# Four leading attention units recast in two 64-token halves, in a planned kernel of linear attention and two MoE layers

## The chip, the cores and the metric

The kernel runs on one core of a Trainium2 chip. The metric is the device time of one execution in microseconds (us), the median of several runs. A profile of one further execution is read beside it; its times count from the start of the profiled span.

## What is computed

```python
def _attn_ref(q, k, v):                      # q, k, v: (2, 8, 768, 64), float32
    ...
    for t in range(S):
        state = gamma[None, :, None, None] * state + np.einsum('bhd,bhe->bhde', k[:, :, t], v[:, :, t])
        y[:, :, t] = scale * np.einsum('bhd,bhde->bhe', q[:, :, t], state)
...
def _moe_ref(x, w_in, w_out):                # x: (1536, 512), w_in: (512, 2048), w_out: (2048, 512)
    h = x @ w_in
    g = np.maximum(h, 0.0) + np.log1p(np.exp(-np.abs(h)))
    return (g @ w_out).astype(np.float32)
...
def _moe2_ref(x, w_in, w_out):
    h = x @ w_in
    relu6 = np.clip(h + 3.0, 0.0, 6.0)
    return ((h * relu6 / 6.0) @ w_out).astype(np.float32)
```

The attention output, turned to (1536, 512), is x of the first layer, whose output is x of the second. The weights come as float64; the kernel turns their 64-bit words into float32 itself.

## The kernel before

**Units.** Attention is cut into 12 units of 128 tokens (all 8 heads), six per batch. Units 0 to 3 (`START`, line 158) give the first 512 tokens, which is the first chunk of x; they stand at the head of the program, and no GEMM can begin before all four are done. Units 4 to 11 run later, two at a time, between GEMMs. A unit's steps on TensorE are named in the planner's table (line 280): Tk and Tq transpose k and q with the identity; S makes the scores, D the product of k and v that feeds the running state, I the part of the output inside the unit, C the part that the carried state adds. In units 0 to 3, S is 8 matmuls of 64 x 128 x 128 (one per head), and I and D 8 each; unit 0 has no C (`attend`, lines 677 to 741). The later units, in pairs, halve their 128 tokens and use 64 x 64 x 64 matmuls, one on each quadrant of the array: `pair`, lines 743 to 829. There the state is added up twice per unit, to a middle state and an end state, and C multiplies both.

Between TensorE's steps, ScalarE (ACT) copies kT out of PSUM and rounds x to `x_hi` (line 738); VectorE (DVE) scales q and v (`qT`, `vs`), masks the scores (`pw`), adds up the state (`st`), reads two columns between two accumulations (`seen`), and makes the low part `x_lo` (line 739).

**Weights.** A block of weights takes one load of raw words (512 KB, tile `raw`) and a row of steps (`Words.made`, line 392): ACT `bits` (`cv<-raw,half`), `sign` (`cv<-raw`) and `scale` (`raw<-raw`), DVE clamp (`raw<-raw`, one or two instructions) and merge (`cv<-raw,cv`), ACT rounding to the high part (`w<-cv`) and DVE the low part (`w<-cv,w`). This text calls the blocks raw_0, raw_1, ... in the order of their loads; the first four go to the weight tiles w_77, w_78, w_79, w_80, and raw_4 to w_81. The buffers number the other way: `raw_0_68` holds raw_0 and later a sixth block, raw_5, and so on.

**GEMMs.** A G1 is twelve 128 x 128 x 512 matmuls of three products (high times high, high times low, low times high), a G2 the same with the second weights. Behind a G1, ACT copies `g` out of PSUM and the softplus follows on DVE and ACT, up to `hi` and `lo`, which the G2 of that block reads.

**Order.** A planner (`Plan.run`, line 75) writes the whole program down in order: each step has a cost, a due time, what it must follow and the buffers it takes, and it picks the next step per engine by earliest start and due time. Due times come from the list of TensorE steps and their costs (lines 284 to 327). A load may carry `hold`, a planned time before which it isn't placed; `HOLD` (line 171) is added to it for the later units (line 627). The chip knows neither: each engine runs its instructions in the written order and waits on semaphores. All loads of the head and the ramp go through SP's queue.

```python
 284      pe = [("Tk", 0), ("Tq", 0)]
 285      for u in range(START):
 286          pe += [("S", u)] + [("C", u)] * (u % (S // P) > 0) + [("D", u)] + ([("Tk", u + 1), ("Tq", u + 1)] if u + 1 < START else []) + [("I", u)]
```

Of the kernel before, what the change touches and what calls it, by code (L numbers as in the profile page):

```python
# [10 lines left out]
F32 = mybir.dt.float32  # L11
# [7 lines left out]
P = 128  # L19
# [126 lines left out]
def kernel(ctx, tc, q, k, v, w1_in, w1_out, w2_in, w2_out, table, out):  # L146
# [7 lines left out]
    C = P  # L154
# [16 lines left out]
    HOLD = 7.0  # L171
# [108 lines left out]
    cost = {"Tk": 0.46, "Tq": 0.46, "S": 0.60, "D": 0.60, "C": 0.98, "I": 0.60, "S0": 0.97, "D0": 0.57, "I0": 0.97, "C0": 0.97, "SS": 1.3, "DD": 1.25, "II": 1.3, "CC": 2.0, "G1": GEMM, "G2": GEMM, "unit": UNIT}  # L280
# [4 lines left out]
    for u in range(START):  # L285
        pe += [("S", u)] + [("C", u)] * (u % (S // P) > 0) + [("D", u)] + ([("Tk", u + 1), ("Tq", u + 1)] if u + 1 < START else []) + [("I", u)]
# [118 lines left out]
    def weight(o, f, number):  # L405
# [19 lines left out]
        t5 = x.made(use - tail, begin + 15 if number < 1 else use - tail - 8.0, 1.45 if o else 1.5 if number < EARLY else 1.75, [x.raw_k], BY_ACT(number))  # L425
# [176 lines left out]
    def attend(u):  # L602
# [71 lines left out]
        o = [("o", u)]  # L674
        dk = ("ds", u)

        def scores(g):
            for p in range(NP):
                nc.tensor.matmul(bank(sc[g])[:, p, :], tile_of("kT")[part[g], p, :], tile_of("qT")[part[g], p, :])

        def all_scores(x):
            for p in range(NP)[ps(x)]:
                for g in range(2):
                    nc.tensor.matmul(bank(sc[g])[:, p, :], tile_of("kT")[part[g], p, :], tile_of("qT")[part[g], p, :])

        def masked(g):
            return lambda: nc.vector.tensor_tensor(tile_of("pw")[:, g], bank(sc[g]),
                                                   full.rearrange("p (n t) -> p n t", n=1).to_broadcast([P, NP, C]), ALU.mult)

        def product():  # L690
            for p in range(NP):
                for g in range(2):
                    nc.tensor.matmul(banks[part[g], nc.slot[dk][1], p * D:(p + 1) * D], tile_of("k")[:, 2 * p + g, :], tile_of("vs")[:, 2 * p + g, :])
# [516 lines left out]
```

## Time and profile before

| what | value |
|---|---|
| time, median of 3 runs | 565.89 us (565.6 to 568.1) |
| the profiled execution's own time | 566.38 us |
| its span, first to last instruction | 564.6 us |
| TensorE (PE) busy | 555.7 us, 98% of the span |
| VectorE (DVE) busy | 438.8 us, 78% |
| ScalarE (ACT) busy | 367.2 us, 65% |
| DMA moved | 100.51 MB, mean 178 GB/s |
| granted TensorE clock | full in all 40 slices |

PE busy counts pipelined matmuls whose ends are modelled, so it tells where PE had work, not how well it was used. The shares are means over very different stages: the head (about 26 us), the ramp in which the first weight blocks are made, and the long middle. Where an edit touches the head alone, the rows of the head and of the ramp behind it are the ones to read.

### The profile page before, as it was taken

To read this page: it belongs to the slowest core of one execution; us is meant where nothing else is said; L and a number is where in the kernel's file an instruction comes from. 1 tells how busy PE (TensorE), PEld (TensorE's weight loads), DVE (VectorE), ACT (ScalarE), POOL (GpSimd) and SP (SyncE) were. 2 spreads that over 40 slices of the span, in tenths; PEclk is the share of its full clock that TensorE was granted. 3 is DMA by queue.
4 is the path that set the end of the run, shared out by engine and by line. 5 is a ranking of instruction groups with operands and counts; after the bars stand their busy time and mean duration, and the time that the engine had idled before them with its cause. 6 is when DMAs were issued, how large, how long until landed. Compare 5 with 4: busy or idle time off the path is not lost.

```text
span 564.6 us, 9538 instructions
## 1 busy us (share of the span) xinstructions
PE 555.7 (98%) x3685; PEld 477.1 (84%) x3685; DVE 438.8 (78%) x778; ACT 367.2 (65%) x600; POOL 6.0 (1%) x13
## 2 busy tenths in 40 slices
PE   7999999999999999999999999999999999999997
PEld 6787888888888888888888899889998899988895
DVE  5999988889699778989998875846888887854343
ACT  4698999998574545576977943548688865432220
POOL 0000000000000000000000000000000000000000
PEclk9999999999999999999999999999999999999999
DMA  9997999996211226796936622151757652226003
GB/s 202 283 268 257 271 280 284 323 253 212 80 56 61 71 93 206 227 320 239 326 157 231 238 90 75 57 205 37 253 195 240 245 186 76 74 89 247 1 0 113
DMA packets 80477, 100.51 MB, mean 178 GB/s; under 512 B 41008, under 2 KB 57648, under 8 KB 80432
## 3 DMA queue, kind: packets, MB, share of 16 engines
q1 hardware_dynamic: 79424, 98.45, 54.1%
q0 software_dynamic: 720, 1.31, 1.4%
q8 instruction: 29, 0.48, 0.3%
q10 hardware_dynamic: 288, 0.14, 0.1%
q14 instruction: 16, 0.13, 0.1%
HBM read 74.98 MB, written 23.59 MB: 175 GB/s over the span
## 4 chain that ended last, share of the span: by engine, by line
PE 82%; DVE 8%; DMA 5%; ACT 3%; issue 1%; SPq 0%; DVEq 0%; ACTq 0%
PE banks L45 82%; DMA raw<-in_moe_w_in_dram 2%; DVE lo L45 2%; DVE g L45 1%; ACT cv L45 1%; DMA g<-stash_h 1%; DMA raw<-in_moe_w_out_dram 1%; DVE raw L45 1%; DVE xf L45 1%; DMA v<-in_v_dram 1%; ACT raw L45 1%; DVE cv L45 1%; DVE e L45 1%; ACT hi L45 1%; DVE w L45 0%
## 5 line engine op out<-in xcount | busy, mean ns | idle before, releaser
L45 PE MATMUL banks<-w,parts 128*128 128x512 f32 x579 | 136.7, 390 | 0.0
L45 PEld LDWEIGHTS banks<-w,parts 128*128 128x128 f32 x579 | 108.0, 188 | 21.3
L45 PE MATMUL banks<-hi,w 128*128 128x512 f32 x384 | 124.9, 393 | 0.0
L45 PE MATMUL banks<-xf,w 128*128 128x384 f32 x672 | 123.3, 337 | 0.4 <-DVE c L45 0.4
L45 PEld LDWEIGHTS banks<-xf,w 128*128 128x128 f32 x672 | 118.2, 188 | 3.6 <-DVE c L45 0.7
L45 PEld LDWEIGHTS banks<-hi,w 128*128 128x128 f32 x384 | 72.1, 188 | 15.2
L45 PE MATMUL banks<-xl,w 128*128 128x512 f32 x342 | 80.8, 391 | 0.0
L45 PEld LDWEIGHTS banks<-xl,w 128*128 128x128 f32 x342 | 63.8, 188 | 13.4
L45 PE MATMUL banks<-lo,w 128*128 128x512 f32 x192 | 74.8, 390 | 0.0
L45 ACT ACTIVATE e<-c,three 128x384 f32<-128x384 f32 (+1 forms) x32 | 24.6, 770 | 47.1 <-DVE c L45 46.8
L45 ACT ACTIVATE cv<-raw,half 128x512 uint32<-128x512 uint32 x64 | 48.4, 760 | 7.5 <-DMA raw<-in_moe_w_in_dram 5.0
L45 ACT ACTIVATE cv<-raw 128x512 f16<-128x512 int32 x64 | 50.2, 791 | 1.3
L45 ACT ACTIVATE e<-e 128x512 f32<-128x512 f32 x48 | 30.1, 628 | 22.9 <-DVE e L45 22.7
L45 DVE SCALAR_TENSOR_TENSOR cv<-raw,cv 128x512 uint32<-128x512 uint32 x64 | 43.8, 688 | 1.1
L45 PE MATMUL banks<-x_hi,w 128*128 128x512 f32 x128 | 42.5, 399 | 1.3 <-ACT x_hi L45 1.3
L45 PEld LDWEIGHTS banks<-lo,w 128*128 128x128 f32 x192 | 36.1, 188 | 7.0
L45 DVE TENSOR_SCALAR raw<-raw 128x512 f32<-128x512 f32 x76 | 32.0, 424 | 11.3 <-ACT raw L45 10.4
L45 ACT ACTIVATE parts<-c 128x768 fp32r<-128x768 f32 x32 | 27.0, 844 | 18.8 <-DVE c L45 18.8
L45 DVE TENSOR_TENSOR c<-total,banks 128x384 f32<-128x384 f32 x16 | 8.9, 554 | 35.1 <-PE banks L45 34.9
L45 DVE TENSOR_TENSOR parts<-c,parts 128x768 fp32r<-128x768 f32 x32 | 30.6, 957 | 7.0 <-ACT parts L45 6.5
L45 DVE SCALAR_TENSOR_TENSOR g<-g,e 128x512 f32<-128x512 f32 x48 | 32.8, 686 | 4.0 <-ACT e L45 3.8
L45 DVE TENSOR_TENSOR lo<-g,hi 128x512 fp32r<-128x512 f32 x48 | 32.8, 685 | 3.7 <-ACT hi L45 3.4
(95 smaller groups left out, 683.5 us busy)
## 6 DMA issues: line engine op xcount, KB each, us to landing
raw<-in_moe_w_in_dram SPq DMA_DIRECT2D x32, 512.0 KB, 5.7
raw<-in_moe_w_out_dram SPq DMA_DIRECT2D x32, 512.0 KB, 5.7
w<-stash_out SPq DMA_DIRECT2D x32, 512.0 KB, 5.3
stash_out<-raw SPq DMA_DIRECT2D x16, 512.0 KB, 3.4
w<-parts_out SPq DMA_DIRECT2D x14, 512.0 KB, 5.8
parts_out<-w SPq DMA_DIRECT2D x8, 512.0 KB, 5.2
stash_h<-hs SPq DMA_DIRECT2D x16, 256.0 KB, 2.0
g<-stash_h SPq DMA_DIRECT2D x16, 256.0 KB, 4.8
```

The source lines that it names most:

```text
L45: return self.plan.tc.keep_in_program_order(getattr(self.engine, op)(*args, **kwargs))
```

## The change

It makes six edits. (1) Units 0 to 3 go through the code of the pairs (now `group`), one unit at a time: halves of 64 tokens, quadrant matmuls, one mask instruction of 512 columns per unit instead of two, a middle state and one more state addition per unit; I comes first and C accumulates onto it, in unit 0 too (for its second half). (2) The planner's costs and TensorE list follow. (3) The low part of x is written over the two-bank form right behind the rounding. (4) `HOLD` falls from 7 to 4. (5) The load of raw_0 gets a due time 10 us later among the loads of the head. (6) Unit 3's last state scaling is due 15 us later, and its qT is preferred.

```diff
-    HOLD = 7.0
+    HOLD = 4.0
...
-    cost = {... "S": 0.60, "D": 0.60, "C": 0.98, "I": 0.60, "S0": 0.97, "D0": 0.57, "I0": 0.97, "C0": 0.97, ...}
+    cost = {... "S": 0.62, "D": 0.62, "C": 1.02, "I": 0.62, ...}
...
-        pe += [("S", u)] + [("C", u)] * (u % (S // P) > 0) + [("D", u)] + ([("Tk", u + 1), ("Tq", u + 1)] if u + 1 < START else []) + [("I", u)]
+        pe += [("S", u), ("D", u)] + ([("Tk", u + 1), ("Tq", u + 1)] if u + 1 < START else []) + [("I", u), ("C", u)]
...
-        t += cost.get(key[0] + "0" if key[0] in "SDIC" and key[-1] < START else "", cost[key[0]])
+        t += cost[key[0]] / (1 + (key == ("C", 0)))
...
-        t5 = x.made(use - tail, begin + 15 if number < 1 else use - tail - 8.0, ...)
+        t5 = x.made(use - tail, begin + 25 if number < 1 else use - tail - 8.0, ...)
...
-        if u >= START:
-            ready["in", u] = kt[0], qt[0], vs, ik[0]
-            if u % 2:
-                pair(u - 1, task)
-            return
...
+        ready["in", u] = kt, qt, vs, ik
+        if u in [START - 1]:
+            for t in qt:
+                t.ahead = 0.6
+        if u < START:
+            group([u], task)
+        elif u % 2:
+            group([u - 1, u], task)
...
-        def all_scores(x):
-            for p in range(NP)[ps(x)]:
-                for g in range(2):
-                    nc.tensor.matmul(bank(sc[g])[:, p, :], tile_of("kT")[part[g], p, :], tile_of("qT")[part[g], p, :])
...
+        def scores(ps):
             for x, w in enumerate(us):
+                for p in ps:
                     for j in range(2):
                         for g in range(2):
                             nc.tensor.matmul(sub(sc, g, x)[part[j], p, :], at_slot(("kT", w))[part[g], p, part[j]], at_slot(("qT", w))[part[g], p, part[j]])
...
-                then = ready["end", w] = task("DVE", 0.42, faded, [then, ready["t"]], d["DD"] + 2.2 + 1.2 * x, give=[("end", w)])
+                then = ready["end", w] = task("DVE", 0.42, faded, [then, ready["t"]], d[E] + 2.2 + 1.2 * x + 15 * (w == START - 1), give=[("end", w)])
...
+        if head:
+            def x_at(part):
+                return split(x_of(part, 0)[:, :, u * C:(u + 1) * C])
+
+            need = min(due["G1", 0], d[I] + 12.0)
+            o2 = task("ACT", PSX, lambda: nc.scalar.activation(x_at("hi"), both(o, 0), AF.Copy), [c], need - 1.5, give=o)
+            o3 = task("DVE", PSX, lambda: nc.vector.tensor_tensor(x_at("lo"), both(o, 0), x_at("hi").bitcast(F32), ALU.subtract), [o2], need - 0.8, give=o)
+            ready["x", u] = [o2, o3]
+            return
```

**ACT ahead of the first GEMM.** These are the rows up to the rounding of unit 3's x, and of the first two weight blocks. Before, from the rounding of unit 2's x on:

```order
L45 ACTIVATE x_hi_291<-banks 128x4x128
L45 ACTIVATE cv_1_74<-raw_1_69,half 128x512
L45 ACTIVATE cv_1_74<-raw_1_69 128x512
L45 ACTIVATE raw_1_69<-raw_1_69 128x512
L45 ACTIVATE cv_2_75<-raw_2_70,half 128x512
L45 ACTIVATE cv_2_75<-raw_2_70 128x512
L45 ACTIVATE x_hi_291<-banks 128x4x128
L45 ACTIVATE w_78<-cv_1_74 128x512
```

and now:

```order
L45 ACTIVATE x_hi_343<-banks 128x2x4x64
L45 ACTIVATE cv_1_74<-raw_1_69,half 128x512
L45 ACTIVATE cv_1_74<-raw_1_69 128x512
L45 ACTIVATE raw_1_69<-raw_1_69 128x512
L45 ACTIVATE cv_2_75<-raw_2_70,half 128x512
L45 ACTIVATE w_77<-cv_0_73 128x512
L45 ACTIVATE x_hi_343<-banks 128x2x4x64
L45 ACTIVATE w_78<-cv_1_74 128x512
```

The three steps of raw_1 and the first of raw_2 stay ahead of unit 3's rounding; the second of raw_2 has moved behind it, and the rounding of w_77, which stood ahead of unit 2's, is in its place.

**SP's loads.** From unit 1's v to the sixth weight block, before:

```order
L45 DMA v_1_141<-in_v_dram 128x8x64
L45 DMA raw_0_68<-in_moe_w_in_dram 128x4x256
...
L45 DMA v_3_152<-in_v_dram 128x8x64
L45 DMA raw_1_69<-in_moe_w_in_dram 128x4x256
L45 DMA raw_2_70<-in_moe_w_in_dram 128x4x256
L45 DMA words_in_112<-cv_0_73 128x512
L45 DMA raw_3_71<-in_moe_w_out_dram 128x1024
L45 DMA raw_4_72<-in_moe_w_in_dram 128x4x256
L45 DMA raw_0_68<-in_moe_w_out_dram 128x1024
L45 DMA k_0_137<-in_k_dram 128x8x64
L45 DMA q_0_134<-in_q_dram 128x8x64
```

and now, from unit 2's v:

```order
L45 DMA v_2_142<-in_v_dram 128x8x64
L45 DMA raw_0_68<-in_moe_w_in_dram 128x4x256
...
L45 DMA raw_1_69<-in_moe_w_in_dram 128x4x256
L45 DMA raw_2_70<-in_moe_w_in_dram 128x4x256
L45 DMA k_0_137<-in_k_dram 128x8x64
L45 DMA q_0_134<-in_q_dram 128x8x64
L45 DMA raw_3_71<-in_moe_w_out_dram 128x1024
L45 DMA raw_4_72<-in_moe_w_in_dram 128x4x256
L45 DMA v_0_140<-in_v_dram 128x8x64
L45 DMA k_1_138<-in_k_dram 128x8x64
L45 DMA q_1_135<-in_q_dram 128x8x64
L45 DMA raw_0_68<-in_moe_w_out_dram 128x1024
```

raw_0 has moved behind unit 2's three loads, with unit 3's three still behind it. raw_1 and raw_2 keep their place. k and q of unit 4 (in the buffers `k_0`, `q_0`) now stand ahead of raw_3, and v of unit 4 with k and q of unit 5 ahead of raw_5; the store `words_in_112` has gone behind them.

**The first G2, on PE and DVE.** PE from the end of unit 3 into the ramp, in pieces of the difference (k_0 is unit 4's k, k_1 and q_1 are unit 5's):

```order
+L45 MATMUL banks<-qT_1_146,st_167 64x64 x8
 L45 MATMUL banks<-ident,k_0_137 128x128 x4
+L45 MATMUL banks<-x_hi_343,w_77 128x512 x8
...
-L45 MATMUL banks<-x_hi_291,w_81 128x512
...
+L45 MATMUL banks<-x_hi_343,w_79 128x512
 L45 MATMUL banks<-ident,k_1_138 128x128 x4
+L45 MATMUL banks<-ident,q_1_135 128x128 x4
 L45 MATMUL banks<-hi_94,w_80 128x512
 L45 MATMUL banks<-lo_96,w_80 128x512
...
+L45 MATMUL banks<-x_hi_343,w_81 128x512
```

DVE up to the low part that this G2 reads, before:

```order
L45 TENSOR_SCALAR e_90<-g_91 128x512
L45 TENSOR_SCALAR raw_4_72<-raw_4_72 128x512 x2
L45 TENSOR_TENSOR w_80<-cv_3_76,w_80 128x512
L45 SCALAR_TENSOR_TENSOR cv_0_73<-raw_4_72,cv_0_73 128x512
L45 SCALAR_TENSOR_TENSOR g_91<-g_91,e_90 128x512
L45 TENSOR_SCALAR e_89<-g_92 128x512
L45 TENSOR_TENSOR w_81<-cv_0_73,w_81 128x512
L45 TENSOR_TENSOR lo_96<-g_91,hi_94 128x512
```

and now:

```order
L45 TENSOR_SCALAR e_90<-g_91 128x512
L45 TENSOR_TENSOR vs_0_147<-v_0_140,small 128x512
L45 TENSOR_TENSOR w_80<-cv_3_76,w_80 128x512
L45 TENSOR_SCALAR e_89<-g_92 128x512
L45 SCALAR_TENSOR_TENSOR g_91<-g_91,e_90 128x512
L45 TENSOR_TENSOR qT_0_145<-banks,tq_sb 128x512
L45 TENSOR_SCALAR raw_4_72<-raw_4_72 128x512 x2
L45 SCALAR_TENSOR_TENSOR cv_3_76<-raw_4_72,cv_3_76 128x512
L45 TENSOR_TENSOR lo_96<-g_91,hi_94 128x512
```

On PE, Tk of unit 4 has moved from behind two GEMMs to ahead of the first, and the G2 of w_80 (behind Tk and Tq of unit 5) to ahead of the G1 of w_81. On DVE its low part `lo_96` still stands last, behind raw_4's clamps and merge, and behind `vs` and `qT` of unit 4, which came later before.

## Rows read from the trace of the kernel before

**Rows 1.** Stages: us, then busy us per engine; last PEclk, DMA share, GB/s
```profile
12.00:26.00 14.00, 13.03 (x208) 11.09 (x206) 13.15 (x28) 9.02 (x14) 0.00 (x0) 1.00 1.06 265
...
26.00:60.00 34.00, 33.70 (x369) 27.38 (x370) 32.28 (x65) 31.66 (x54) 0.39 (x1) 1.00 0.90 262
60.00:200.00 140.00, 140.00 (x1299) 114.91 (x1298) 117.69 (x209) 110.68 (x186) 4.48 (x5) 1.00 0.63 189
```

**Rows 2.** Timeline of PE, unit 3 and the first GEMM (start, us, ...)
```profile
21.33 1.16 PE L45 MATMUL banks<-qT,kT 64*128 64x128 f32 x16
22.42 1.09 PE L45 MATMUL banks<-qT,st 64*64 64x128 f32 x16
23.44 0.69 PE L45 MATMUL banks<-vs,k 128*64 128x64 f32 x16
23.96 1.07 PE L45 MATMUL banks<-pw,vs 128*64 128x128 f32 x16
26.30 2.11 PE L45 MATMUL banks<-x_hi,w 128*128 128x512 f32 x8 [1.27 <-ACT x_hi L45]
```

**Rows 3.** Timeline of PE, S and C of the pair of units 4 and 5
```profile
44.82 1.16 PE L45 MATMUL banks<-qT,kT 64*64 64x64 f32 x64
...
56.94 2.08 PE L45 MATMUL banks<-qT,st 64*64 64x64 f32 x64
```

**Rows 4.** Timeline of ACT, ahead of the first GEMM and at the first softplus
```profile
22.02 0.77 ACT L45 ACTIVATE cv<-raw,half 128x512 uint32<-128x512 uint32 x1
...
25.03 0.79 ACT L45 ACTIVATE cv<-raw 128x512 f16<-128x512 int32 x1
25.68 0.57 ACT L45 ACTIVATE x_hi<-banks 128x512 fp32r<-128x512 f32 x1
26.14 0.62 ACT L45 ACTIVATE w<-cv 128x512 fp32r<-128x512 f32 x1
26.66 0.67 ACT L45 ACTIVATE raw<-raw 128x512 f32<-128x512 f32 x1
...
34.60 0.63 ACT L45 ACTIVATE hi<-g 128x512 fp32r<-128x512 f32 x1
```

**Rows 5.** Timeline of SP: issues of raw_1 with raw_2, and of raw_3
```profile
16.05 1.79 SPq L45 DMA_DIRECT2D raw<-in_moe_w_in_dram  x2
...
18.45 0.43 SPq L45 DMA_DIRECT2D raw<-in_moe_w_out_dram  x1
```

**Rows 6.** DMA issues at 16.0 and at 18.4 us: KB, us to landing
```profile
raw<-in_moe_w_in_dram SPq DMA_DIRECT2D x1, 512.0 KB, 5.9
...
raw<-in_moe_w_out_dram SPq DMA_DIRECT2D x1, 512.0 KB, 7.0
```

**Rows 7.** Timeline of PE in the ramp: Tk of unit 5, first G2, third G2
```profile
38.28 0.66 PE L45 MATMUL banks<-ident,k 128*128 128x128 f32 x4
38.70 0.48 PE L45 MATMUL banks<-hi,w 128*128 128x512 f32 x1
...
50.28 0.39 PE L45 MATMUL banks<-lo,w 128*128 128x512 f32 x1
```

**Rows 8.** Timeline of DVE in the ramp: first and third low part, mask, states
```profile
35.42 0.68 DVE L45 TENSOR_TENSOR lo<-g,hi 128x512 fp32r<-128x512 f32 x1
36.02 0.42 DVE L45 TENSOR_SCALAR raw<-raw 128x512 f32<-128x512 f32 x1
...
46.18 1.22 DVE L45 TENSOR_TENSOR pw<-banks,small 128x1024 f32<-128x1024 f32 x1
...
49.19 0.68 DVE L45 TENSOR_TENSOR lo<-g,hi 128x512 fp32r<-128x512 f32 x1
...
50.13 0.86 DVE L45 TENSOR_TENSOR st<-st,banks 128x256 f32<-128x256 f32 x2
```

**Rows 9.** Two stretches: around the first GEMM, and in the ramp
```profile
24.00:28.00 4.00, 2.73 (x29) 2.21 (x24) 3.85 (x9) 3.97 (x7) 0.00 (x0) 1.00 1.08 368
...
40.00:50.00 10.00, 10.00 (x149) 7.97 (x147) 10.00 (x20) 9.62 (x17) 0.00 (x0) 1.00 0.86 304
```

More of the change, by code (lines that the diff above doesn't have):

```diff
@@ L686, in masked @@
[L686 to L693, printed above, removed]
-        def inner():
-            for p in range(NP):
-                for g in range(2):
-                    nc.tensor.matmul(bank(o[0])[part[g], p, :], tile_of("vs")[:, 2 * p + g, :], tile_of("pw")[:, g, p, :],
-                                     **(dict(start=(p == 0), stop=(p == NP - 1)) if first else dict(start=False, stop=True, skip_group_check=True)))
@@ L701, in between @@
-        def between():
-            nc.vector.tensor_copy(seen, bank(o[0])[:, 0, :2])
-        def carry():
-            for p in range(NP):
-                for g in range(2):
-                    nc.tensor.matmul(bank(o[0])[part[g], p, :], at_slot(("end", u - 1))[part[g], p, :], tile_of("qT")[part[g], p, :],
-                                     start=(p == 0), stop=(p == NP - 1))
-        def added():
-            return banks[:, nc.slot[dk][1], :NP * D].rearrange("p (n t) -> p n t", n=NP)
-        def total():
-            nc.vector.tensor_tensor(at_slot(("end", u)), at_slot(("end", u - 1)), added(), ALU.add)
@@ L716, in faded @@
-        def faded():
-            nc.vector.tensor_tensor(at_slot(("end", u)), added() if first else at_slot(("end", u)),
-                                    tc_sb.rearrange("p (n o) -> p n o", o=1).to_broadcast([P, NP, D]), ALU.mult)
-        s = [task("PE", cost["S0"] / parts, lambda x=x: all_scores(x), [kt[x], qt[x]], d["S"] + x / 10, take=[] if x else [("bank", x) for x in sc], give=[("kT", u)] + [("qT", u)] * first) for x in range(parts)]
-        pt = [task("DVE", PSX, masked(g), s, d["I"] - 1.8 + g * 0.6, take=[] if g else own("pw"), give=[sc[g]]) for g in range(2)]
@@ L732, in attend @@
-        c = task("PE", cost["I0"], inner, pt + [vs, n], d["I"], take=[("bank", o[0])] if first else [],
-                 give=[("pw", u), ("vs", u)])
-        def x_at(part):
-            return x_of(part, 0)[:, :, u * C:(u + 1) * C]
-        need = min(due["G1", 0], d["I"] + 12.0)
-        o2 = task("ACT", PSX, lambda: nc.scalar.activation(x_at("hi"), bank(o[0]), AF.Copy), [c], need - 1.5, give=o)
-        o3 = task("DVE", PSX, lambda: nc.vector.tensor_tensor(x_at("lo"), bank(o[0]), x_at("hi").bitcast(F32), ALU.subtract), [o2],
-                  need - 0.8, give=o)
@@ L741, in attend, with group @@
-        ready["x", u] = [o2, o3]
-    def pair(u, task):
+        ready["in", u] = kt, qt, vs, ik
[6 more added lines that the diff above has]
+            group([u - 1, u], task)
+    def group(us, task):
+        u, head = us[0], us[0] < START
         ph = int(u >= FIRST)
-        us = u, u + 1
-        d = {n: due[n, u] for n in ("SS", "DD", "II", "CC")}
+        S, E, I, R = "SDIC" if head else ("SS", "DD", "II", "CC")
+        d = {n: due[n, u] for n in (S, E, I, R)}
```

53 lines of the change are left out of this document (20 added, 33 removed).

## The prediction

> **What bounds the kernel now.** I read the busy time by stage first [rows 1]: from 60 us to 200 us TensorE has work for 140.00 of 140.00 us, from 26 to 60 us for 33.70 of 34.00. Once the first GEMM has begun, PE never stands still for long, and the end comes one PE program after that start. So the change can move the end in two ways: by when the first GEMM begins, and by PE stalls that it takes away or makes behind it. Second, the timeline of PE in the head [rows 2]: the first GEMM begins at 26.30, after 1.27 us without work, and what it waited for was ACT's rounding of unit 3's x, not PE. Third, ACT [rows 4]: that rounding ran at 25.68, behind a row of weight steps that began at 22.02. Fourth, why not sooner: the load of raw_1, the first of those steps' input, was issued at 16.05 [rows 5] and took 5.9 us [rows 6], so it landed at 21.95. The head therefore ends on this chain: landing of raw_1, ACT's queue, x_hi, first GEMM. PE's own head work was nearly as long (busy 13.03 of 14 us [rows 1]), but was not the last to arrive. Fifth, the ramp: from 40 to 50 us DVE was busy for 10.00 of 10.00 us and ACT for 9.62 [rows 9]; behind the start stands a second limit, close below PE.
>
> **PE's work in the head.** From start to start a unit took S 1.09, C 1.02, D 0.52, and I 1.07 by its duration [rows 2], together 3.70. In the pair's form S of two units lasts 1.16 and C 2.08 [rows 3]; one unit is half: S 0.58, C 1.04, and I and D at 0.58, since they have as many quadrant matmuls as S. That is 2.78, a saving of 0.92 for each of units 1 to 3, 2.8 in all. Unit 0 loses 2.68 (S, D, I) and gets 1.74 plus half a C (0.52): 0.4 less. PE's head shrinks by 3.2 us. What covers it: nothing on PE; the time turns into waiting, since the chain above does not run through it. DVE's head work changes little: one mask of 512 columns less per unit, one state addition more.
>
> **The start of the first GEMM.** raw_1 keeps its place in SP's order, behind the loads of all four units and raw_0. I leave its landing at 21.95. ACT's queue then holds the same four weight steps, and in place of raw_2's sign step (25.03 to 25.68, 0.65) the rounding of w_77, which took 0.52 of the queue in w_78's case (26.14 to 26.66) [rows 4]. x_hi comes 0.13 sooner, a little more as the rounding need not wait for the step before it: 0.2. w_77's low part on DVE follows its rounding by one instruction of 0.68, as the low parts in [rows 8], ends near 26.3, and is needed by the second matmul. I take -0.2, start 26.1. Bounds: -3.2, PE's whole saving, if raw_1 landed so early that it held nothing up (the first rival); +1.1, if raw_1 took the 7.0 us of raw_3 [rows 6].
>
> **Tk of unit 4** now fits into the gap ahead of the first GEMM; its 0.42 (Tk of unit 5 runs from 38.28 to 38.70 [rows 7]) is gone from the stage that counts: -0.42. If unit 4's k landed after 25.6 it would be worth less; it is the next load but one after raw_1, so I keep it. Both ends: 0 and -0.42.
>
> **The first G2.** From 26.30 to 38.28 PE did four GEMMs, Tk and Tq [rows 2, 7], 2.79 a GEMM if a transpose costs 0.42. Its place was at 38.70. It now stands one G1 earlier and one Tq later: 38.70 - 0.62 - 2.79 + 0.42 = 35.7, its second matmul, which reads the low part, 0.3 later, at 36.0. That low part was made at 35.42 to 36.10 [rows 8], its high part began at 34.60 [rows 4]. ACT's queue up to that high part holds two steps less and two more, so I leave it there. But raw_4's sign step now stands right ahead of it, and on DVE raw_4's two clamps and merge stand between: from 34.7, 0.42, 0.34 and 0.60, then 0.68: begun at 36.1, ready at 36.8. (On DVE the next instruction begins 0.08 ahead of an end, as 35.42 to 36.02 against 0.68 shows, so I count 0.60 for 0.68 and 0.34 for 0.42.) PE waits 0.8. Bounds: 0 (before, DVE was 2.9 us ahead of PE here, 36.10 against 39.0) and 1.3 (one more 0.60 late on DVE).
>
> **The mask and D of units 4 and 5.** S of the pair now stands ahead of the second G2 instead of behind it, and D behind that G2, so PE reaches D where S ended before (44.82 + 1.09): 45.9 - 0.62 + 0.8 = 46.1. The mask began 10.76 us after the first low part (46.18 against 35.42 [rows 8]), with DVE full; now three instructions of 0.60 and two of 0.34 fewer lie between and one of 0.60 more, 1.9 us less, so it runs from 36.1 + 8.9 = 45.0 to 46.2. D waits 0.1. Bounds 0 and 1.0 (DVE waiting for ACT on the way).
>
> **The third G2** needs its low part, made at 49.19 to 49.87; PE read it at 50.28 [rows 7, 8], only 0.4 later. Now two state additions (0.86 [rows 8]) and w_84's low part stand ahead of it on DVE: mask 45.0 + 1.14, then 0.60, 0.34, 0.68, 0.60, 0.60 and 0.86 give 49.8, ready at 50.5. PE arrives at 50.28 - 0.62 + 0.8 + 0.1 = 50.56. No further wait, and none to gain either: a PE that came sooner would stop here. Behind this point PE has the same list in both kernels, and DVE has 22 us free in the next 140 [rows 1].
>
> **The low part of x, HOLD and the rest.** `x_lo` costs the same 128 x 512; unit 3's is behind the first eight matmuls, as before: 0. HOLD is nothing to the chip; what it moves are the five loads ahead of raw_3 and raw_5. For raw_3 that is 512 KB more and a store of 256 KB less; at 262 GB/s [rows 1] it lands 1.0 later than 18.45 + 7.0 = 25.45 [rows 5, 6], at 26.4. ACT gets to it four steps behind x_hi (0.46, 0.52 and raw_2's last two, 0.79 and 0.55, from 25.5), at about 27.8: hidden, with 1.4 us left. The later state scaling of unit 3 is needed first by C of unit 4: 0.
>
> **Sum:** -0.2 - 0.42 + 0.8 + 0.1 = +0.3 on the profiled execution, 566.38 + 0.3 = 566.7. The median shown is 565.89, 0.5 below it, so the forecast is **566.2 us**. A measurement of this kernel can tell about 0.5% (2.8 us) from no change; this is no change.
>
> **A rule weighed.** By PE's rows alone the sum would be 566.38 - 3.2 - 0.4, in the median 562.3. The Trainium skill, TensorEngine Tiling (Array Packing), section PSUM Bottleneck, says that tiling makes TensorE faster but not the emptying of PSUM, which may become the limit. By that rule the sum would keep nothing of the 3.2. The trace agrees in the result, not in the cause: ACT's queue ahead of x_hi is full of weight steps [rows 4], PSUM copies are a small part of it.
>
> **Rivals.** *PE-bound head:* raw_1 lands sooner, ACT and DVE run ahead, and PE's saving reaches the end: 562.3. For: PE was busy 13.03 of 14 us in the head. Against: the same bytes stand ahead of raw_1 with the DMA engines full (share 1.06), and DVE in the ramp stops PE at the third G2. Each us that raw_1 lands sooner gives about one. 0.09.
>
> *Unit 4 and 5's loads in the weights' way (slower):* raw_3 lands not at 26.4 but behind ACT. It decides from 27.8 for raw_3, and from about 35 (behind the first softplus's high part) for raw_5, which has all five loads ahead of it (1.3 MB, 5 us at 262 GB/s, less 1 for the store). Behind that point ACT (31.66 of 34 us busy) has no slack and every us late is a us at the end. For: the DMA engines were 0.90 busy from 26 to 60 us [rows 1], so nothing makes up for a late load. Against: 1.4 us of margin. Price if raw_3 is 3 us later than my 26.4: 1.6, and raw_5 another 1.4: 569.2. 0.13.
>
> *The clock (slower):* PE now waits more between 17 and 26 us. In the row with the most idle time, 2.73 of 4.00 us busy, the granted clock was 1.00, that is 2.4 GHz [rows 9]. The Trainium skill, TensorE: Matmul & The Clock Gate, section HAM oscillation, says that idle gaps can send the clock down to 1.2 GHz. By that rule, one GEMM at half the clock takes 2.79 more: 569.0. No row here shows a fall, and the new gaps are shorter pieces of the same kind. 0.03.
>
> That the change doesn't do what it says is no rival: the order of the instructions shows every piece moved.
>
> **Numbers.** Forecast case, PE stopped by ACT and DVE in the ramp, 0.75, its own range 564.3 to 568.2 from the bounds of its terms. Faster by over 0.5%: 0.09 of the PE-bound head plus 0.01 of the forecast case, 0.10. Slower by over 0.5%: 0.10 of the loads and 0.02 of the clock, 0.12. Same: 0.78. The range 563.8 to 568.8 leaves out the far ends of both sides.
>
> **What would show it.** First GEMM at 25.8 to 26.4, waiting for ACT's x_hi or DVE's w; PE idle for 2 us or more between 17 and 26; Tk of unit 4 ahead of it; a PE stall of 0.5 to 1.0 at the first G2 with `lo` as releaser, a smaller one at D of units 4 and 5; the low part of the third G2 done at 50 to 51. Wrong if the first GEMM begins before 25, or if ACT waits for a raw load between 26 and 40.

## The result and the profile after

| | before | after |
|---|---|---|
| median of 8 runs each | 567.77 us (565.60 to 568.83) | 570.97 us (569.19 to 571.75) |
| ratio, 95% interval | | 1.0057 (1.0037 to 1.0078) |
| span of the profiled execution | 564.6 us | 569.3 us |
| first GEMM begins at | 26.30 [rows 2] | 29.94 |
| mean granted clock of that execution | 1.000 | 0.994 |

The kernel became slower by 0.57%, a little more than a measurement can tell from nothing, and the forecast of no change was wrong: 570.97 lies above its range. Of the 4.8 us between the forecast of 566.2 and 570.97, 1.9 are the base: the forecast started from 565.89, the median of three runs of before, and eight runs give 567.77. The rest is the change. A second series of the same kernel gave 1.0048 (1.0030 to 1.0067).

What PE waited for in the whole execution after (us in total, times, longest):

```profile
PE banks L45 <- issue: 4.7, 2, 3.8
...
PE banks L45 <- DVE lo L45: 0.7, 1, 0.7
```

The first line has no counterpart before. "issue" means that PE stood still and the profile shows nothing that it waited for: no semaphore, no DMA. The timeline of PE in the head after tells where; it answers to [rows 2]:

```profile
17.48 0.33 PE L45 MATMUL banks<-pw,vs 64*64 64x64 f32 x4
18.73 0.68 PE L45 MATMUL banks<-pw,vs 64*64 64x64 f32 x28 [0.93 <-issue]
19.35 0.66 PE L45 MATMUL banks<-ident,q 128*128 128x128 f32 x4
19.93 1.15 PE L45 MATMUL banks<-qT,st 64*64 64x64 f32 x32
20.88 0.69 PE L45 MATMUL banks<-qT,kT 64*64 64x64 f32 x32
21.38 0.69 PE L45 MATMUL banks<-vs,k 64*64 64x64 f32 x32
25.86 1.13 PE L45 MATMUL banks<-pw,vs 64*64 64x64 f32 x32 [3.78 <-issue]
27.27 1.97 PE L45 MATMUL banks<-qT,st 64*64 64x64 f32 x32 [0.28 <-DVE seen L45]
29.17 1.11 PE L45 MATMUL banks<-ident,k 128*128 128x128 f32 x4
29.94 2.56 PE L45 MATMUL banks<-x_hi,w 128*128 128x512 f32 x8
```

The first stall stands in the middle of unit 2's I, between two matmuls of one group with the same tiles; no mask or state can be late there. Between it and the second lie 28 + 4 + 32 + 32 + 32 = 128 matmuls. (The x of a row counts what the trace records, two for a float32 matmul of the program in S, D, I and C; all counts here are of that kind.) With its weight load each is a pair, so 256 instructions lie between the stalls. The stall then spread: DVE's `seen` waited for PE, the merge of a weight block stood behind it on DVE, and the roundings behind that on ACT. DVE and ACT after, same stretch:

```profile
27.05 0.16 DVE L45 COPY seen<-banks 128x2 f32<-128x2 f32 x1 [3.81 <-PE banks L45]
27.46 0.69 DVE L45 SCALAR_TENSOR_TENSOR cv<-raw,cv 128x512 uint32<-128x512 uint32 x1
28.18 0.63 ACT L45 ACTIVATE w<-cv 128x512 fp32r<-128x512 f32 x1 [3.65 <-DVE cv L45]
29.29 0.60 ACT L45 ACTIVATE x_hi<-banks 128x512 fp32r<-128x512 f32 x1 [0.48 <-PE banks L45]
```

And the clock fell. Stretches after, as in [rows 9] (stretch, its length, busy us and counts of PE, PEld, DVE, ACT and POOL; then PEclk, DMA share, GB/s):

```profile
22.00:26.00 4.00, 0.22 (x11) 0.15 (x8) 1.25 (x3) 2.46 (x4) 0.00 (x0) 0.76 1.15 282
26.00:30.00 4.00, 3.72 (x69) 3.36 (x69) 2.81 (x7) 1.34 (x3) 0.00 (x0) 0.50 1.12 267
30.00:34.00 4.00, 4.00 (x18) 3.27 (x17) 2.89 (x6) 3.94 (x7) 0.00 (x0) 0.88 0.91 210
```

PE had 0.22 us of work in the four ahead of 26, and the next four ran at 0.50, the lower level of 1.2 GHz: C took 1.97 instead of 1.15, the first eight matmuls of the GEMM 2.56 instead of 2.11 [rows 2].

**What came in by DMA at that time.** The profile page's list of queues has two whose kind is "instruction". q14 has 16 packets in both kernels; q8 has 29 of 16 KB before and 31 after (the columns are packets, MB, share of the 16 engines):

```profile
q8 instruction: 29, 0.48, 0.3%
...
q8 instruction: 31, 0.51, 0.4%
```

PE's rows grew from 3685 to 3941 matmuls, by 256, which is two packets of 128 pairs. So q8 carries PE's code, 128 pairs a packet. The packet for the code behind 25.86 began to move between 22.9 and 23.2 (at 23.04), the queues of that stretch after:

```profile
q1 hardware_dynamic: 273, 0.07, 130.0%
q8 instruction: 1, 0.02, 27.3%
```

It took 1.3 us, and PE went on 1.5 us behind its end. The first stall ended in the same way: a packet from 15.90 to 17.19, PE at 18.73. PE had gone over to the block ahead, the one just in front of that code, at 18.73. From there to 22.9 the data queue alone had the engines (98.4% of all sixteen in the mean; in the first us the slices show 0.2 to 0.9). In the kernel before, a packet was nearly as late without a cost: it began at 25.0, and by the same count PE had gone over at 21.3, but the block it was in lasted to 39.7. The Trainium skill, Runtime: NRT & Kernel Launch, section Instruction fetch mechanics, says that code comes in blocks of 16 KiB, 256 instructions, fetched through a DMA queue of the sequencer's own while the block ahead of it is executed, and that crossing a block is mostly hidden. The trace agrees with the size; hidden it was not.

### The profile page after: what moved, and what is told of

It is laid out like the page before. It is cut to its first block, busy times and chain, and to the rows that moved or that the text cites. A ratio compares the mean times of both kernels' runs of the same rounds, so it can differ in the third digit from the quotient of the medians.

```text
span 569.3 us, 10063 instructions
## 1 busy us (share of the span) xinstructions
PE 556.8 (98%) x3941; PEld 478.0 (84%) x3941; DVE 439.2 (77%) x780; ACT 368.1 (65%) x600; POOL 5.9 (1%) x13
## 4 chain that ended last, share of the span: by engine, by line
PE 85%; DMA 4%; DVE 4%; ACT 3%; SPq 2%; issue 2%; DVEq 0%
PE banks L45 85%; SPq L45 2%; DMA raw<-in_moe_w_out_dram 2%; ACT cv L45 2%; DVE raw L45 1%; DMA k<-in_k_dram 1%; DMA stash_out<-raw 1%; DVE cv L45 0%; ACT raw L45 0%; DMA out_dram<-ob 0%; DVE w L45 0%; ACT e L45 0%; DVE ob L45 0%; ACT w L45 0%; ACT parts L45 0%
## 5 line engine op out<-in xcount | busy, mean ns | idle before, releaser
L45 PEld LDWEIGHTS banks<-w,parts 128*128 128x128 f32 x579 | 108.1, 188 | 21.3
L45 ACT ACTIVATE hi<-g 128x512 fp32r<-128x512 f32 x48 | 30.1, 627 | 16.8 <-PE banks L45 8.5
L45 ACT ACTIVATE raw<-raw 128x512 f32<-128x512 f32 x52 | 34.5, 669 | 0.9
```

The source lines that it names most:

```text
L45: return self.plan.tc.keep_in_program_order(getattr(self.engine, op)(*args, **kwargs))
```

## The experiments

**Theory A:** the new form has 136 pairs a unit instead of 72 and runs through a block faster than the next can come in behind the data; PE stands still for code, and the clock falls in the gap. **Rival L:** the other loads cost. **Rival S:** an operand, mask or state is late ahead of I.

All ratios are to the kernel before, run beside each kernel on the same chip. "At 70 us" is how far PE's GEMM matmuls stand behind their counterparts in the first profiled execution of before, at its 70 us; "end" compares the spans.

| run | ratio (95%) | `issue`, us | first GEMM | at 70 us | end |
|---|---|---|---|---|---|
| the change | 1.0057 (1.0037 to 1.0078) | 4.7 | 29.94 | +5.0 | +4.7 |
| after_again | 1.0048 (1.0030 to 1.0067) | 3.0 | 28.18 | +3.2 | +4.3 |
| before_again | single run, 567.60 us | none | 26.24 | -0.1 | +1.2 |
| loads_alone | 1.0062 (1.0041 to 1.0083) | none | 28.20 | +2.7 | +6.3 |
| hold_alone | 1.0042 (1.0024 to 1.0060) | none | 26.44 | +0.8 | +3.0 |
| raw0_alone | 1.0033 (1.0014 to 1.0051) | none | 27.01 | +2.4 | +3.0 |
| form_alone | 1.0085 (1.0058 to 1.0111) | 3.0 | 28.10 | +3.3 | +5.0 |
| shift_12 | single run, 577.79 us | 2.9 | 34.76 | +9.7 | +11.4 |
| more_pairs | single run, 588.57 us | 5.5 | 45.35 | +19.2 | +22.2 |
| late_loads | 1.0148 (1.0107 to 1.0189) | 4.4 | 28.88 | +7.7 | +11.6 |
| gate | single run, 570.48 us | 0.7 | 26.10 | +3.2 | +4.1 |
| gate_hold55 | 1.0051 (1.0034 to 1.0068) | 0.7 | 26.69 | +2.6 | +5.0 |
| gate_hold7 | 1.0139 (1.0105 to 1.0172) | 0.5 | 26.33 | +7.1 | +11.5 |
| one_carry | 1.0029 (1.0009 to 1.0048) | 0.8 | 27.08 | +2.4 | +3.4 |
| few_pairs | 1.0029 (1.0008 to 1.0049) | none | 26.07 | +2.2 | +3.0 |
| few_old_loads | 1.0065 (1.0043 to 1.0088) | none | 28.52 | +5.8 | +7.1 |
| few_warm | 0.9981 (0.9963 to 0.9998) | none | 27.75 | +2.6 | +1.8 |

### Where the stall sits: the same twice, a shift, and the old form with more code

after_again is the changed kernel unedited.

> The changed kernel once more. Theory A: stalls put down to 'issue' at the same two matmuls (after the fourth of unit 2's inner products, ahead of unit 3's), 3.5 to 5.5 us in sum, granted clock 0.45 to 0.9 between 22 and 34 us, first GEMM at 29 to 30.8; time 2.5 to 4.5 us above before. If the stall was an accident of one execution: no such waits and a first GEMM near 26.2.

```profile
18.66 0.68 PE L45 MATMUL banks<-pw,vs 64*64 64x64 f32 x28 [0.29 <-issue]
...
24.68 0.69 PE L45 MATMUL banks<-pw,vs 64*64 64x64 f32 x32 [2.68 <-issue]
```

The timeline of PE in that run: the same two matmuls, so no accident. The stalls were smaller than expected (3.0 us against 3.5 to 5.5, first GEMM at 28.18 against 29 to 30.8): how long PE waits differs between executions, where it waits doesn't.

```diff
     awake(4)
+    for i in range(12):
+        nc.tensor.matmul(idle[:, i % NP, :8], tq_sb[:, 0], tq_sb[:, 0, :8])
```

> The changed kernel with 12 more tiny matmuls (8 columns each, results unused) right behind the first four at the start, some 0.4 us of work 1 us into the span, where PE waits anyway. Theory A: the stalls sit at counted instructions, so both come 12 matmuls sooner in the order: the first after 28 of the 32 of unit 2's state products (not within its inner products), the second after 20 of the 32 of unit 3's state products, each put down to 'issue'; the second again 3 to 4.5 us. Rival S, an engine's or a semaphore's lateness: the stalls stay at unit 2's and unit 3's inner products.

The 12 matmuls are 24 in the trace (32 rows of `tq_sb` instead of 8), so the stalls should come 24 sooner, not 12. The timeline of PE in that run, two units with the stall in each:

```profile
17.85 0.62 PE L45 MATMUL banks<-vs,k 64*64 64x64 f32 x25
18.73 0.34 PE L45 MATMUL banks<-vs,k 64*64 64x64 f32 x7 [0.26 <-issue]
19.00 0.66 PE L45 MATMUL banks<-ident,k 128*128 128x128 f32 x4
19.59 0.69 PE L45 MATMUL banks<-pw,vs 64*64 64x64 f32 x32
20.21 0.66 PE L45 MATMUL banks<-ident,q 128*128 128x128 f32 x4
20.80 1.15 PE L45 MATMUL banks<-qT,st 64*64 64x64 f32 x32
21.93 0.69 PE L45 MATMUL banks<-qT,kT 64*64 64x64 f32 x32
22.43 0.46 PE L45 MATMUL banks<-vs,k 64*64 64x64 f32 x16
25.26 0.46 PE L45 MATMUL banks<-vs,k 64*64 64x64 f32 x16 [2.36 <-issue]
```

These are units 1 and 2. The stall of unit 2 moved from behind the fourth matmul of I to behind the sixteenth of D: back over 4 of I, 4 of Tk and 16 of D, 24 in all. The one ahead of unit 3's I moved behind the eighth of its D, again 24 back, but with 0.23 us instead of the 3 to 4.5 foretold. D waits for no mask; rival S falls. The time of this run says nothing: the added matmuls were 128 wide in their weights and took 4.9 us, and the whole head began late.

more_pairs goes the other way, in the old form of the head:

```diff
         def all_scores(x):
+            for n in range(64 // parts):
+                nc.tensor.matmul(bank(sc[n % 2])[:8, 0, :8], tile_of("kT")[part[n % 2], ps(x).start, :8], tile_of("qT")[part[n % 2], ps(x).start, :8])
             for p in range(NP)[ps(x)]:
```

> The kernel before, with 64 tiny products (8 rows, 8 columns, overwritten by the scores right behind them) ahead of each of units 0 to 3's scores: 128 pairs more a unit, 200 instead of 72, some 2 to 3 us more work a unit. Theory A: the old form too then runs out of code: waits put down to 'issue' on PE, 2 us or more in sum, the places 128 pairs apart. Rival (the stall belongs to the quadrant form, to its waits or its masks): no 'issue' wait over 0.3 us; PE only later by its added work.

```profile
20.47 1.97 PE L45 MATMUL banks<-qT,st 64*64 64x128 f32 x15 [1.96 <-issue]
...
38.70 2.08 PE L45 MATMUL banks<-qT,kT 64*128 64x128 f32 x16 [3.53 <-issue]
```

PE in that run: without the new form, without a change of the loads, the stall is there, once in the middle of C. The stall belongs to the amount of code.

Counted from the first matmul of a trace, all 17 `issue` waits of the ten runs that have any sit ahead of one of four places, whatever matmul stands there: number 222, 349 (350 in more_pairs), 477 and 733, 127 to 128 apart or twice that. And each ends 1.1 to 1.6 us behind the end of a packet on q8. That leaves no operand, mask or state as the cause of these waits.

### Fewer pairs, the same work

```diff
+                if head:
+                    j, g = 1, 0
+                    nc.tensor.matmul(banks[part[g], nc.slot[o[j]][1], :].rearrange("p (n t) -> p n t", n=4), at_slot(("mid", w))[part[g], 0, :], at_slot(("qT", w))[part[g], :4, :], start=False, stop=True, skip_group_check=True)
+                    continue
                 for j in range(int(first[x]), 2):
```

> The changed kernel, but the carry of units 0 to 3 (16 and three times 32 matmuls of 64 columns, 0.95 to 1.15 us each unit) is one matmul of 512 columns with about the same time; what it leaves out: the carried state's share of the outputs of units 0 to 3. PE has about the same work in 109 instructions pairs less. Theory A: the block boundary moves 13 matmuls into unit 3's scores and its packet is asked for a block sooner: 'issue' waits on PE under 1 us in sum, granted clock 1.00 up to the first GEMM, first GEMM at 25.9 to 26.6, time 565.5 to 568 (against before within 0.3%). Rival S (an operand, a mask or a state is late ahead of unit 3's inner products) and rival L (loads): the wait of 3 to 4 us ahead of unit 3's inner products stays, time 2 to 5 us above before.

```profile
20.86 0.57 PE L45 MATMUL banks<-qT,kT 64*64 64x64 f32 x22 [0.77 <-issue]
```

One stall of 0.77 was left, not 3.78, and it sat behind the tenth matmul of unit 3's scores (13 foretold). But the clock fell all the same (0.994 in the mean, 1.00 foretold), the first GEMM came at 27.08 instead of 25.9 to 26.6, and the time kept its bound in the ratio (0.29%), not in us (569.58 against 568). few_pairs goes on from there:

```diff
         def inner():
             for x, w in enumerate(us):
+                if head:
+                    for g in range(2):
+                        for j in range(2):
+                            nc.tensor.matmul(sub(o, j, x)[part[g]], at_slot(("vs", w))[part[j], g, :], weights()[part[j], g], start=True, stop=True, skip_group_check=True)
+                    continue
```

> The run with one carry, and besides the inner products of units 0 to 3 as 4 matmuls of 256 columns instead of 16 of 64 (every head pair with the first one's operands), so about the same or less time on PE in some 82 pairs of weight load and matmul a unit instead of 136 (before: 72). What it leaves out: most of the inner products and of the carry of units 0 to 3. Theory A: no wait put down to 'issue' over 0.3 us, granted clock 1.00 in 16 to 34 us, first GEMM at 25.9 to 26.8, PE within 1.5 us of before at 60 us; time 566.5 to 569.5, what is left over before being the loads' own cost (0.3 to 0.4% in the runs that change one number of them). If the other edits, not the supply of code, cost the time: first GEMM later than 27.5, time as the changed kernel's, 570 to 572.

No `issue` wait is left, and the first GEMM begins at 26.07, where the prediction had put it. The time (569.41) kept the forecast of theory A, but the clock and the place at 60 us (2.15 behind, at most 1.5 foretold) didn't; stretches of that run, and its first GEMM:

```profile
24.00:28.00 4.00, 2.81 (x10) 2.00 (x10) 3.44 (x8) 3.97 (x8) 0.00 (x0) 0.74 0.98 301
28.00:32.00 4.00, 4.00 (x16) 3.25 (x15) 3.13 (x7) 3.78 (x7) 0.00 (x0) 0.83 1.22 220
```

```profile
26.07 3.61 PE L45 MATMUL banks<-x_hi,w 128*128 128x512 f32 x8 [0.76 <-ACT x_hi L45]
```

Here no code was late. PE had short waits of its own (0.34, 0.24, 0.33, 0.42 and 0.76 us behind 20) and began the GEMM at half the clock: 3.61 us for eight matmuls that took 2.11 before. In before the wait ahead of the GEMM was longer, 1.27 in one piece, and the clock stayed up. few_warm fills the last of these gaps:

```diff
+            if s == 0 and 0 in only:
+                for _ in range(2):
+                    nc.tensor.matmul(h, tq_sb[:, 0], tq_sb.rearrange("p n t -> p (n t)"), start=True, stop=True, skip_group_check=True)
             for n, (kk, a, b) in enumerate(sorted(ops, ...)):
```

> The run with few pairs, and two products of 512 columns (results overwritten) ahead of the first GEMM, some 1.7 us in PE's gap there. If the clock's fall in that gap costs (the run with few pairs took 3.61 us for the first eight matmuls of the first GEMM, at 2.11 before): granted clock 1.00 in 24 to 32 us, those eight at 2.1 to 2.4 us, PE at 60 us 0.6 to 1.4 us nearer to before than the 2.15 of the run with few pairs, 0.1 to 0.25% less time. If not: the same clock, or the same time at 60 us.

The profiled execution missed: the clock was already down when the filler began (0.57 in 24 to 28 us), the GEMM began at 27.75 behind it, and PE was no nearer at 70 us. Over twelve runs the time did fall, by more than foretold: 567.47, from 0.29% above before to 0.19% below, two intervals that do not meet, if only by 0.1%; the two series ran on different chips, each beside its own before. Seven of the twelve had a mean granted clock of 1.000; of few_pairs' twelve none had (0.993 to 0.999). But these seven took 567.39 in the median and the other five 567.54, so these means don't explain the gain. In the two profiles few_warm ends 1.2 sooner only because few_pairs waits 1.5 us for `base` behind 250 us. That the filler pays is what the medians say; how it pays isn't shown.

### Does the packet wait behind data?

late_loads was to hold back all loads from the third weight block on until unit 3's scores were done.

```diff
...
+        if us == [START - 1]:
+            ready["gate"] = s[-1]
+            for f in order[2:]:
+                T["F", f].after.append(s[-1])
```

> The changed kernel, but the third weight block and all loads behind it (units 4 on too) may begin only when unit 3's scores are done, near 21 us. At 18.5 us, when PE goes over to the block of code ahead, only the second weight block's load is then under way. Theory Q (a code packet waits behind the data already asked for): the packet that started at 22.8 starts at 20.8 to 21.8, unit 3's inner products begin at 24.0 to 24.9 instead of 25.86, the first GEMM at 28.0 to 29.2. Rival F (the packet's wait is fixed, or PE asks for it late): packet at 22.3 or later, unit 3's inner products at 25.4 or later. The time itself is left wide, 567.5 to 573, since all later weights begin 3 to 4 us later.

It didn't hold them: what a step "follows" orders the planner's list and makes no wait on the chip, so the third block was issued at 17.8 as before, and only the order behind it changed. The packet's start (23.0 in the rows, 22.8 in the time of the expectations, which runs 0.25 early) therefore says nothing on theory Q; of the 1.5%, 0.5 are the changed kernel's own, and the rest shows what a worse order of the loads costs. gate makes a real wait, with a small store that SP can't issue before qT of unit 3 is made:

```diff
...
+            ready["gate"] = nc.add("SP", 0.1, lambda: nc.sync.dma_start(out=kept("gate", 8), in_=at_slot(("qT", START - 1))[:, 0, :8]), [iv, *qt], begin + 40)
+            for f in order[2:]:
+                T["F", f].after.append(ready["gate"])
```

> The changed kernel, where SP first has to write out a few words of unit 3's turned and scaled q (made near 20.7 us) before it may ask for the third weight block and all that is behind it, so that when PE goes over to the next block of code at 18.5 to 19 us only the second weight block's load is in flight. This makes the wait that the run called late_loads did not make. Theory Q (the code packet waits behind data already asked for): the packet that started at 22.8 starts at 20.8 to 21.8, unit 3's inner products at 23.8 to 24.9 instead of 25.86. Rival F (the packet's wait does not hang on the data): packet at 22.3 or later. The time is not what is looked at: the later weights begin 3 to 4 us later, 570 to 580.

Queues in that run from 20.7 to 21.0 us, and PE behind them:

```profile
q1 hardware_dynamic: 82, 0.07, 71.6%
q8 instruction: 1, 0.02, 21.1%
```

```profile
23.04 0.69 PE L45 MATMUL banks<-pw,vs 64*64 64x64 f32 x32 [0.76 <-DVE st L45]
24.02 1.15 PE L45 MATMUL banks<-qT,st 64*64 64x64 f32 x32 [0.28 <-DVE seen L45]
26.10 2.41 PE L45 MATMUL banks<-x_hi,w 128*128 128x512 f32 x8 [0.93 <-ACT x_hi L45]
```

The packet moved 2.2 us sooner, at 20.81, while the second weight block was running out (it landed at 21.66). I began at 23.04, sooner than theory Q foretold, and waited for DVE, not for code; the clock stayed at 1.00, and the first GEMM began at 26.10, 3.84 ahead of the changed kernel. Theory Q holds for these 2.2 us; the packet still began 1.9 us behind PE's step into the block ahead (18.92), and this run doesn't divide that. But at 70 us PE was 3.2 behind again. Two more orders of the loads with the same gate (hold 7 and 5.5 instead of 4) asked whether that can be kept.

> The run called gate, with hold 7 in place of 4, so that behind the third weight block the fourth and fifth come first and the loads of units 4 and 5 behind them, as in the kernel before. Theory A (the late code packet is what the change lost by): no 'issue' wait ahead of unit 3's inner products (the first one, 0.3 to 0.9 us in unit 2's, stays), granted clock 1.00 up to 34 us, first GEMM at 26.0 to 26.6, PE at most 2 us behind before at 60 us, time 566.5 to 569.5, faster than the changed kernel by 1.5 to 4 us. Rival W (what the gate wins is lost again on the weights that it holds back): PE 2.5 us or more behind before at 60 us, time 570 or more.

> The same with hold 5.5: behind the third weight block the fourth, then unit 4's k and q, then the fifth. Theory A: as with hold 7, first GEMM at 26.0 to 26.6, time 566.5 to 569.5. Rival W: waits for w of 0.5 us or more between 30 and 45 us, PE 2.5 us or more behind before at 60 us, time 570 or more.

It can't, in these two. PE in the one with hold 7, then in the one with 5.5:

```profile
38.93 0.63 PE L45 MATMUL banks<-ident,k 128*128 128x128 f32 x4 [2.96 <-DMA k<-in_k_dram]
```

```profile
38.65 0.50 PE L45 MATMUL banks<-lo,w 128*128 128x512 f32 x1 [1.29 <-DVE lo L45]
```

First GEMM at 26.33 and 26.69, no `issue` wait behind 19 us, and yet 1.0139 and 1.0051. Rival W was right for both in the time and in the place at 60 us (4.9 and 2.6 behind); the waits for w that it named for hold 5.5 were waits for low parts, `x_lo` and `lo`, of 1.3 each. The bytes that let the code through come 3 us later (in gate the third weight block lands at 26.01 instead of 23.16), and the ramp has no slack for them. With hold 7 the clock fell too, at 39.4 us.

### The loads

The two numbers on loads in the kernel before, together (loads_alone), and one by one (hold_alone: `HOLD = 4.0`; raw0_alone: `begin + 25`); and the change without them (form_alone).

> The kernel before with only the two numbers on loads changed (hold 4 instead of 7 for units 4 on, the first weight block's load due 10 us later); the matmuls of the head stay as they were. Theory A, TensorE ran out of instructions: its code comes in packets of 16 KB, 128 matmuls and their weight loads each, and the head's 128-wide form uses one packet in 7 to 8 us, so nothing stalls: no wait put down to 'issue' on PE over 0.3 us, first GEMM at 26.0 to 27.0, time within 0.25% of before. Rival L, the earlier loads of units 4 and 5 are what cost: first GEMM later than 28, time 2 to 5 us above before, as in the changed kernel.

> The changed kernel with the two numbers on loads put back (hold 7, first weight block's load due 10 us sooner); the new form of the head's matmuls and the order of the low parts stay. Theory A: the 'issue' waits on PE stay, at the same two matmuls (after the 4th of unit 2's inner products and ahead of unit 3's), 2 to 5 us in sum; the time 2 to 5 us above before. Rival L: no such waits, first GEMM near 26.2, time within 0.25% of before. Should the traffic on the queues set how long a packet takes, the sum of the waits changes by up to 2 us either way.

> The kernel before with hold 4 instead of 7 alone; SP's order is the same up to the first weights and differs from there to the end of the program. Theory A (the stalled code packets are the whole cost): first GEMM at 26.0 to 27, time within 0.25% of before. Theory H (the other order of the loads costs by itself, by late weights of the second layer that ACT waits for with PE's products behind them): first GEMM the same, but PE waits of 2 to 4 us in sum on base, part or hs between 250 and 450 us, time 2 to 4 us above before.

> The kernel before with the first weight block's load due 10 us later alone; on SP it moves behind unit 2's three loads. Theory A: time within 0.25% of before, first GEMM at 26.0 to 27. Theory R (in the old form of the head the later first weight block is what the first GEMM waits for): first GEMM at 27.5 to 28.5 with ACT w as releaser, 1.2 to 2.2 us above before in the end; PE waits behind 60 us under 1 us in sum.

Both sides missed something. No `issue` wait appears in the old form, as theory A said, but the time rose by 0.62%, 0.42% and 0.33%; loads_alone kept rival L's first GEMM (28.20) and its time. hold_alone leaves the first GEMM at 26.44; what PE waited for there between 250 and 400 us (0.4 us in that stretch before):

```profile
PE banks L45 <- DVE part L45: 1.1, 1, 1.1
PE banks L45 <- ACT between L45: 0.4, 1, 0.4
```

That is theory H in kind, below its size (2 to 4 us). raw0_alone begins its GEMM 0.7 later, waiting for the rounded first weight block (theory R in kind, again below its size):

```profile
27.01 0.50 PE L45 MATMUL banks<-x_hi,w 128*128 128x512 f32 x1 [1.56 <-ACT w L45]
```

form_alone has its stalls at two counted places 256 pairs apart (0.74 in unit 1's I, where unit 2's had been foretold, and 2.30 ahead of unit 3's), and with 1.0085 a worse ratio than the whole change; it lost 6.2 us, more than the 2 to 5 of theory A. So the loads cost in the old form, and by the medians they help in the new one, but there the intervals overlap (1.0058 to 1.0111 against 1.0037 to 1.0078). few_old_loads looks at the second half of that without late code:

> The run with few pairs (most of the carry and of the inner products of units 0 to 3 left out), with the two numbers on loads put back to hold 7 and the first weight block 10 us sooner. It splits what is left of the loss when the code stall is gone (0.29%) between the loads and the new form. If the loads hold it: time within 0.2% of before, waits on PE behind 250 us under 1 us. If the form holds it (clock, later low parts): 0.2 to 0.5% above before, and the first GEMM near 26.5 to 28 with the granted clock under 1.00 in some stretch of 16 to 34 us.

1.0065, against 1.0029 with the new loads (on another chip, and here too the intervals touch), and a first GEMM at 28.52: more than either side foretold. ACT, DVE and PE of that run:

```profile
23.29 0.75 ACT L45 ACTIVATE cv<-raw,half 128x512 uint32<-128x512 uint32 x1 [3.70 <-DMA raw<-in_moe_w_in_dram]
...
24.72 0.57 ACT L45 ACTIVATE x_hi<-banks 128x512 fp32r<-128x512 f32 x1
```

```profile
25.32 0.69 DVE L45 TENSOR_TENSOR x_lo<-banks,x_hi 128x512 fp32r<-128x512 f32 x1 [2.20 <-ACT x_hi L45]
25.93 0.15 DVE L45 COPY seen<-banks 128x2 f32<-128x2 f32 x1
```

```profile
26.13 1.07 PE L45 MATMUL banks<-qT,st 64*64 64x512 f32 x2 [3.13 <-DVE seen L45]
```

With the old loads unit 2's rounding stands on ACT behind a weight block that hasn't landed, the low part of x stands on DVE right behind the rounding, `seen` behind that, and C of unit 3 on PE behind `seen`. The clock fell here as well: the first eight matmuls took 3.78. The third edit thus can turn a late weight into a PE stall where the loads aren't moved too.

before_again fixes the scale of all this.

> The kernel before once more, one look. All theories: no 'issue' wait; first GEMM at 26.0 to 27.5; it shows how far two executions of one kernel differ in the head and in the waits behind 250 us (0.4 us of waits there in the first): expected 0 to 2 us.

Two executions of before agree to 0.1 us up to 250 us and then differ by 1.2 (waits on `parts_out` and `base`), so a difference of about 1 us in the last column is nobody's doing.

## Why the prediction was wrong

**The step that failed is the start of the first GEMM**, taken as -0.2 (bounds -3.2 to +1.1) and measured as +3.64, in a second execution +1.88. Its premise was that PE's saved 3.2 us could only turn into waiting for ACT, and that PE would always be ready. PE's work shrank as foretold: from start to start S takes 0.50, D 0.63, I 0.62 and C 0.95, together 2.70 against the 2.78 of the sum, with S and C below its terms and D and I a little above. raw_1 landed at 21.6, against 21.95. With the code out of the way the start is where the step put it: 26.07 in few_pairs, by the path of the forecast (raw_1 landed at 22.04, and ACT was busy from there to x_hi), and 26.10 in gate, by another path and so in part by luck: raw_2 came late there, and ACT stood 0.85 us behind DVE's merge just ahead of w_77 and x_hi. What was missing is a resource that no row of before showed at its limit. Before, a unit of 72 pairs took 4.78 us (16.55 to 21.33, the starts of two S), so a packet of 128 would last 8.5; after, 136 pairs took 4.17 (11.07 to 15.24), so it lasts 3.9. And behind the loads a block took 5.7 us from the start of the one ahead (13.0, counted back 128 pairs, to 18.73) and the next 7.1 (18.73 to 25.86). The order of both kernels' instructions and the q8 line of the profile page of before were there to read.

**The clock** stood as a rival at 0.03, for idle gaps of PE's own. It came, once behind the code stall and, in few_pairs, without one, so the rival named a real mechanism and its chance was far too small. The Trainium skill, TensorE: Matmul & The Clock Gate, section HAM oscillation, says that idle gaps bring it about; after the stalls of the change and after_again the trace agrees (0.50). But not every gap did: form_alone's profiled execution stood 2.30 us and kept 1.00, and its first eight matmuls took 2.11:

```profile
28.10 2.11 PE L45 MATMUL banks<-x_hi,w 128*128 128x512 f32 x8 [0.70 <-ACT x_hi L45]
```

In few_pairs the fall cost 1.5 us on these eight. In form_alone the two runs with a mean clock of 0.998 and 1.000 took 570.66 and 571.38, the four with 0.992 to 0.997 took 573.15 to 573.93.

**Unit 4's Tk** moved ahead of the first GEMM as foretold (29.17), and takes 0.77 there at the lower clock.

**The first G2's low part**, +0.8: the wait is there, 0.67 by DVE `lo`. **D of units 4 and 5**, +0.1: from the last matmul ahead of it to D 0.49 instead of the 0.23 of a running GEMM, so 0.3. **The third G2**, 0: 0.2 (its second matmul 0.39 behind its first, at 54.73). These three were right in kind and near in size:

```profile
41.11 0.50 PE L45 MATMUL banks<-lo,w 128*128 128x512 f32 x1 [0.67 <-DVE lo L45]
...
50.31 0.39 PE L45 MATMUL banks<-hi,w 128*128 128x512 f32 x1
50.80 1.15 PE L45 MATMUL banks<-vs,k 64*64 64x64 f32 x48
```

**HOLD, raw_0 and the low part of x**, 0: in the change itself ACT waits for no weight between 26 and 40 us, so the rival of the late weights did not happen; raw_3 landed at 27.82 instead of 26.4, which took up the 1.4 us of margin, and the late start of the GEMM hid it. But "hidden" was not a property of the loads: in the old form they cost 0.3 to 0.6%, without them the new form loses more by the medians. **"Behind this point PE has the same list"** holds for PE; the loads behind it have another order through the whole program, and PE's waits behind 250 us were 0.4 us before, 0.3 after (1.3 in after_again), none in raw0_alone, 1.5 in hold_alone and 3.2 in loads_alone.

**What is settled and what isn't.** That PE ran out of code, that less data ahead brings the packet 2.2 us sooner, and that 4.1 of the 4.7 us between the two profiles stand at or ahead of the first GEMM's first matmuls is shown. How the 0.5% of the medians divide is less sharp: few pairs alone bring 1.0048 to 1.0057 down to 1.0029 (the intervals overlap), the filler the rest, in a way that no row shows. Every run without the long stall had other edits or another order of the loads, so the clock's share and the ramp's can't be taken apart further. No version that computes the whole result beat the kernel before.

## What to carry to other kernels

Count the instructions of an engine, not only their time: many small matmuls in a stretch where the DMA queues are full can run through their code faster than it arrives, and an `issue` wait in the middle of a group, at places a fixed count apart, is its mark. Where PE isn't the last to arrive, a faster PE gains nothing and may lose: its gaps can cost the clock of the GEMM that follows, as in few_pairs, though they need not, as in form_alone. And a load that is held back to let something through is paid for where it is needed, so look at the ramp behind before calling a queue's slack free.

## What the runs showed of the hardware that was not expected

PE's code comes as one 16 KB packet for 128 pairs of weight load and matmul, on q8. Under load a packet began to move up to 4.3 us after PE went over to the block ahead (18.73 to 23.0); behind 26 us, 28 more packets came in without one `issue` wait. With less data ahead of it, it came 2.2 us sooner, so it had no right of way over the data here. PE went on 1.1 to 1.6 us behind a packet's end. Small quadrant matmuls ran at 16 ns a pair (S, 32 pairs in 0.50 us), so by estimate a block of these alone would be gone in 2 us. And at 26 to 30 us after, PE was busy for 3.72 of 4.00 us at the lower clock: the clock came back only behind that work.
